# Tying weight stores, operand stores and the first operation of each weight conversion to their place in program order

## The chip, the cores and the metric

One core of one Trainium2 chip. The metric is the device time of one execution in microseconds (us), the median of three runs. PE is TensorE, DVE VectorE, ACT ScalarE, POOL GpSimd, SP SyncE, the engine whose only work here is to issue loads.

## The reference, cut to what matters

Three stages follow one another; 4 batches of 768 tokens are the 3072 rows of the last two.

```python
# 1: chunked attention, 8 heads of 64, chunk 32, left 16, right 8, 8 memory keys
scores = scale * q_c @ k_full.T ; a = softmax(scores) ; out = a @ v_full
# 2: x [3072,512], w_in [512,2048], w_out [2048,512]
h = x @ w_in ;  g = h * tanh(log1p(exp(h))) ;  x = g @ w_out
# 3: w_gate, w_val [512,1536], w_out2 [1536,512]
xn = x / sqrt(mean(x*x) + 1e-6) * rms_g
out = (silu(xn @ w_gate) * (xn @ w_val)) @ w_out2
```

The weights arrive as float64.

## The kernel before, in words

**Tiling.** The 3072 rows are 24 attention tiles of 128 rows. Three tiles make a block of 384 rows, two blocks a pair; there are four pairs. A product with `w_in`, or with `w_gate` and `w_val` together, is done for a pair at once by a 2x2 scheme with seven products (`group`, line 510). Its operands are seven tiles `T` per pair and seven parts of a weight slot. Every operand is split into a high and a low part (`split`, line 130: a copy on ACT, a subtraction on DVE or POOL), and each product is three matmuls for each of two contraction steps: 42 matmuls of 384 columns in a group.

**Weights.** A weight tile is loaded by SP as raw float64 halves (`load_raw`, line 119, two buffers `raw`) and converted by the generator `cv_all` (line 148). Its first two operations, lines 158 and 161, are on ACT and read `raw`; DVE goes on in lines 163 to 170. A job "pair" converts two tiles, forms sums on POOL and DVE, and splits into a slot; it has 11 steps. A job "rows" has 4 steps for each tile. `cv_upto(n)` advances the generator to step n at the places where the program calls it: 22 steps (two pairs, 4 tiles) while the first pair's attention is written down, to 55 in the 28 slots of the first four groups, to 88 in the next 56 slots, then none for 56 slots, to 152 in 84 slots, to 218 over the 64 steps of `out1`, to 284 and 332 in the last groups.

**Stages in time.** Attention of pair 0 (6 tiles, lines 342 to 443) comes first: no product exists before it. Then come 32 groups for `w_in` (line 551), where attention of pairs 1 to 3 lies between the products (`slots`, line 722), `out1` (64 steps of 24 matmuls, line 613), 48 groups for gate and value (line 561), and `out2` (line 663).

**Stores.** `w_store` (line 116, called by `keep_w`) writes a converted `w_in` slot to DRAM so that it can be loaded again for a later pair; the program places the eight stores in slots 1, 5, 14, 21, 30, 37, 44 and 51 of the second phase, which has the 56 slots of groups 4 to 11. `keep_x` (line 757) writes the seven `T` tiles of pair 0, in slots 8 to 20 of the first phase, groups 0 to 3. `store` (line 672) writes the result. Other stores go through `store_later` and `flush` (lines 92 to 99). All are issued from ACT's queue.

**What sets the order.** Each engine runs its instructions in one fixed order. That order isn't the one of the program text: a scheduler writes it when the kernel is built, from simulated times (`schedule_with_timeline_sim`, line 19). An instruction whose inputs are ready in that simulation may be put ahead of instructions that stand before it in the text.

Of the kernel before, what the change touches and what calls it, by code (L numbers as in the profile page):

```python
# [8 lines left out]
F32 = mybir.dt.float32  # L9
# [19 lines left out]
def tile_kernel(  # L29
# [13 lines left out]
    out: bass.AP,  # L43
):
    nc = tc.nc
    B, H, S, D = q.shape
    NMEM = mem_k.shape[2]
    NT, DM = out.shape
# [4 lines left out]
    N = 384  # L53
# [10 lines left out]
    wd = {("i", i): nc.dram_tensor(f"wi{i}", (128, SLOT), F32R, kind="Internal").ap()  # L64
          for i in range(F1 // 2)}
# [26 lines left out]
    def store_later(dst, src):  # L92
        late.append((tick[0] + 2, dst, src))

    def flush(all_=False):
        tick[0] += 1
        while late and (all_ or late[0][0] <= tick[0]):
            _, dst, src = late.pop(0)
            nc.scalar.dma_start(out=dst, in_=src)


    def w_slot(u):
        pool = w1p if u < NW1 else w2p[0]
        return pool.tile([128, SLOT], F32R, tag=f"w{u}", name="w")

    wtab, wslot = {}, {}

    def as7(s):
        return s.rearrange("p (a l f) -> p a l f", a=7, l=2)
# [4 lines left out]
        wtab[key] = as7(s)  # L114

    def w_store(key):
        nc.scalar.dma_start(out=wd[key].bitcast(F32), in_=wslot[key].bitcast(F32))

    def load_raw(arr, kind, f):
        raw = rawp.tile([128, 512, 2], I32, tag="raw", name="raw")  # L120
# [9 lines left out]
    def split(src, hi, lo, eng=None):  # L130
        nc.scalar.copy(hi, src)  # L131
        (eng or nc.vector).tensor_tensor(lo, src, hi.bitcast(F32), op=ALU.subtract)  # L132
# [3 lines left out]
    def add_pair(key, arr0, f0, arr1, f1, u, keep, store):  # L136
        jobs.append(("pair", key, [(arr0, "col", f0), (arr1, "col", f1)], u, keep, store))
# [4 lines left out]
    def cv_prefetch(done):  # L142
        flat = [part for job in jobs for part in job[2]]
        while n_load[0] < len(flat) and n_load[0] - done < 2:
            raws.append(load_raw(*flat[n_load[0]]))
            n_load[0] += 1

    def cv_all():

        done = 0  # L150
        for kind, key, parts, u, keep, store in jobs:
            tiles, slot = [], None
            for n in range(len(parts)):
                cv_prefetch(done)
                raw = raws.pop(0)
                a = cap.tile([128, 512], I32, tag="ca", name="ca")
                lr = cvp.tile([128, 512], I32, tag="lr", name="lr")
                nc.scalar.activation(
                    a.bitcast(F32), raw[:, :, 1].bitcast(F32), ACTF.Copy, scale=2.0 ** -112
                )  # L160
                nc.scalar.activation(lr, raw[:, :, 0].bitcast(U32), ACTF.Copy, scale=2.0 ** -29)
                yield
                nc.vector.tensor_scalar(a, a, 3, None, op0=ALU.logical_shift_left)
                nc.vector.scalar_tensor_tensor(  # L164
                    a, raw[:, :, 1], -2 ** 31, a, op0=ALU.bitwise_and, op1=ALU.bitwise_or
                )
                done += 1
                cv_prefetch(done)
                yield
                nc.vector.tensor_tensor(a, a, lr, op=ALU.add)  # L170
                yield
                a = a.bitcast(F32)
                if kind == "pair":
                    tiles.append(a)
                    continue
                if n == 0:
                    slot = w_slot(u)[:, 0:3 * 1024].rearrange("p (a l f) -> p a l f", a=3, l=2)
                w = slot[:, n]
                split(a, w[:, 0, :], w[:, 1, :], nc.gpsimd)
                wtab[key[n]] = w  # L180
                yield
            if kind == "rows":
                continue
            a0, a1 = tiles
            a11, a12, a21, a22 = a0[:, 0:256], a0[:, 256:512], a1[:, 0:256], a1[:, 256:512]
            sm = cvp.tile([128, 4, 256], F32, tag="sm", name="sm")
            s4, s1, s2, s3 = (sm[:, i, :] for i in range(4))
            nc.gpsimd.tensor_tensor(s1, a21, a22, op=ALU.add)
            nc.gpsimd.tensor_tensor(s3, a11, a21, op=ALU.subtract)
            slot = w_slot(u)  # L190
            w = as7(slot)
            def part(i, src):
                cnt = src.shape[-1] // 256
                src = src.rearrange("p (a f) -> p a f", f=256)
                split(src, w[:, i:i + cnt, 0, :], w[:, i:i + cnt, 1, :])
            part(0, a0)
            yield
            nc.vector.tensor_tensor(s2, s1, a11, op=ALU.subtract)
            nc.vector.tensor_tensor(s4, a12, s2, op=ALU.subtract)
            yield  # L200
            part(2, a22)
            yield
            part(3, sm[:, 0:2, :].rearrange("p a f -> p (a f)"))
            yield
            part(5, sm[:, 2:4, :].rearrange("p a f -> p (a f)"))
            if store:
                store_later(wd[key].bitcast(F32), slot.bitcast(F32))
            if keep:
                wtab[key], wslot[key] = w, slot
            yield  # L210
# [449 lines left out]
    def banks2(m):  # L660
        return [bk[(3 * m + r) % 8] for r in range(NSUB)]
# [10 lines left out]
    def store(m, n):  # L672
        for r, ps in enumerate(banks2(m)):
            o = cap.tile([128, 512], I32, tag="ca", name="o").bitcast(F32)
            if r % 2 == 0:
                nc.scalar.copy(o, ps)
            else:
                nc.vector.tensor_copy(o, ps)
            nc.scalar.dma_start(out=out[n * N + 128 * r:n * N + 128 * r + 128, :], in_=o)


    nc.scalar.preload_act_table_set("natural_log_exp_and_others")
# [16 lines left out]
    for f, u in zip(range(0, F2, 3), (7, 1, 2, 3)):  # L699
        fs = range(f, min(f + 3, F2))  # L700
        add_rows([("o2", x) for x in fs], w_out2, fs, u)
    cv[0] = cv_all()

    load_k(0, 0)
# [50 lines left out]
        return lambda: t_pieces(j, xb.pop(2 * j), xb.pop(2 * j + 1), t_new, None, ttab_x)  # L755

    def keep_x(p):
        return lambda: nc.scalar.dma_start(
            out=xt_d[:, p - 1].bitcast(F32), in_=ttab_x[0, p].bitcast(F32)
        )  # L760

    def keep_w(i):
        return lambda: w_store(("i", i))

    bt = slots((att_list(1), 28), (0, 55), tail_of(1),
               {8 + 2 * n: keep_x(p) for n, p in enumerate(ORDER)})
    for i in A:
        group1(0, i, bt)
# [51 lines left out]
    for s, (m, i) in enumerate(steps):  # L820
# [3 lines left out]
        if i == F1 // 2 - 1 and m < NB - 1:  # L824
            assert not pend
            n = order[m]
# [21 lines left out]
    def t_slot():  # L848
        if "x" not in hold:
            hold["x"] = w_slot(2)[:, 0:4 * N].rearrange("p (a b n) -> p a b n", a=2, b=2)  # L850
            return hold["x"]
        u = hold["n"] = hold.get("n", -1) + 1
        if u % 2 == 0:
            hold["s"] = w_slot(3)[:, 0:8 * N].rearrange("p (s a b n) -> p s a b n", s=2, a=2, b=2)
        return hold["s"][:, u % 2]

    p0, pend = rms_pieces(NB - 1, 1, t_slot)
    p0()

    def both():  # L860
        early, rest = t_pieces(0, xn.pop(0), xn.pop(1), t_slot, nt_d[0], {})
        pend.extend(early + rest)
# [41 lines left out]
    for s, (m, i) in enumerate(steps):  # L904
        t = feed.next(s)
        out2(m, i, t)
        if i == F2 // 2 - 1:
            store(m, order[m])
# [30 lines left out]
```

## Time and profile before

| | us |
|---|---|
| median of 3 runs (lowest, highest) | 1333.88 (1332.31, 1336.42) |
| the profiled execution's own time | 1333.24 |
| its span | 1331.5 |
| PE busy in the span | 1227.7 |
| DVE / ACT / POOL busy | 738.1 / 586.8 / 236.1 |

The span runs from the first to the last instruction of the profiled execution. A busy PE is not PE at its peak: matmuls are pipelined, so the count of matmuls in a stretch tells more than its busy time. "DMA share" is the mean busy share of the core's 16 DMA engines.

### The profile page before, as it was taken

The page shows a single profiled execution, that of the slowest core. Times are in us where ns is not written, and L with a number is a line of the kernel's source. Part 1 is how long each engine was busy: PE and PEld are TensorE (multiplying, and loading weights), DVE is VectorE, ACT ScalarE, POOL GpSimd, SP SyncE. Part 2 cuts the span into 40 slices and gives each one's busy share as a digit, 9 for nine tenths or more (in the row PEclk, how much of TensorE's full clock was granted, in tenths as well). Part 3 has the DMA queues.
Part 4 walks back from the last instruction along what each step waited for, and adds up shares of the span by engine and source line. Part 5 has one row for each costly group of instructions (what it writes and reads, how often), then busy time and mean ns, then how long its engine had stood idle before and what let it go on. Part 6 is the DMA issues. An engine that isn't in the chain of part 4 may idle for free.

```text
span 1331.5 us, 23277 instructions
## 1 busy us (share of the span) xinstructions
PE 1227.7 (92%) x9248; PEld 1134.2 (85%) x9248; DVE 738.1 (55%) x1276; ACT 586.8 (44%) x976; POOL 236.1 (18%) x197
## 2 busy tenths in 40 slices
PE   5559989999999879999999999989999999999998
PEld 3348778888899869989999999989999999888887
DVE  5666487363477577764656376955554337422220
ACT  4444355343354468757676344542432224322220
POOL 1002021020053311221212121311321114000000
PEclk9968889979999899999999999989999999999999
DMA  9998469669468697563636949858954553734321
GB/s 236 252 269 273 108 176 339 174 179 281 130 268 300 256 358 236 159 252 104 239 116 230 407 159 413 308 199 335 360 193 171 226 190 113 223 119 143 119 84 48
DMA packets 190637, 291.00 MB, mean 219 GB/s; under 512 B 103744, under 2 KB 152896, under 8 KB 186432
## 3 DMA queue, kind: packets, MB, share of 16 engines
q1 hardware_dynamic: 163600, 182.29, 43.5%
q10 hardware_dynamic: 26928, 107.23, 20.4%
q8 instruction: 72, 1.18, 0.4%
q14 instruction: 37, 0.30, 0.1%
HBM read 182.26 MB, written 107.22 MB: 217 GB/s over the span
## 4 chain that ended last, share of the span: by engine, by line
PE 48%; DMA 10%; DVE 6%; ACT 5%; issue 2%; POOL 1%; ACTq 0%; DVEq 0%; SPq 0%; POOLq 0%
PE bk L506 8%; PE bk L575 8%; PE bk L576 8%; PE bk L577 8%; PE bk L508 8%; PE bk L507 8%; DMA g<-g_scratch 3%; DMA T<-nt_scratch 3%; DVE T L132 2%; ACT T L131 1%; DMA T<-xt_scratch 1%; DVE ca L164 1%; ACT g L598 1%; DMA wg<-w 1%; DMA raw<-in_moe_w_out_dram 1%
## 5 line engine op out<-in xcount | busy, mean ns | idle before, releaser
L506 PE MATMUL bk<-T,w 128*128 128x384 f32 x1120 | 385.3, 348 | 21.1 <-DMA T<-nt_scratch 7.1
L507 PE MATMUL bk<-T,w 128*128 128x384 f32 x1120 | 383.7, 343 | 2.2 <-DVE T L132 2.1
L508 PE MATMUL bk<-T,w 128*128 128x384 f32 x1120 | 377.7, 342 | 0.0
L506 PEld LDWEIGHTS bk<-T,w 128*128 128x128 f32 x1120 | 215.1, 193 | 30.9 <-ACT s L568 6.3
L507 PEld LDWEIGHTS bk<-T,w 128*128 128x128 f32 x1120 | 215.0, 192 | 5.8 <-DVE T L132 4.7
L508 PEld LDWEIGHTS bk<-T,w 128*128 128x128 f32 x1120 | 214.5, 192 | 0.7
L132 DVE TENSOR_TENSOR T<-g,T 128x768 fp32r<-128x768 f32 x112 | 112.6, 1011 | 134.5 <-ACT T L131 134.1
L575 PE MATMUL bk<-T,w 128*128 128x384 f32 x512 | 169.8, 340 | 8.6 <-ACT T L131 8.6
L576 PE MATMUL bk<-T,w 128*128 128x384 f32 x512 | 174.1, 340 | 3.3 <-DVE T L132 3.3
L577 PE MATMUL bk<-T,w 128*128 128x384 f32 x512 | 172.5, 337 | 0.0
L131 ACT CAST T<-g 128x768 fp32r<-128x768 f32 x112 | 91.9, 835 | 108.2 <-PE bk L577 95.4
L575 PE MATMUL bk<-w,T 128*128 128x512 f32 x288 | 112.6, 391 | 0.0
L576 PE MATMUL bk<-w,T 128*128 128x512 f32 x288 | 112.5, 391 | 0.0
L577 PE MATMUL bk<-w,T 128*128 128x512 f32 x288 | 112.2, 391 | 0.0
L533 DVE TENSOR_TENSOR u<-bk,s 128x384 f32<-128x384 f32 x80 | 44.3, 553 | 112.1 <-PE bk L508 112.0
L575 PEld LDWEIGHTS bk<-T,w 128*128 128x128 f32 x512 | 96.2, 189 | 10.8 <-ACT T L131 10.2
L576 PEld LDWEIGHTS bk<-T,w 128*128 128x128 f32 x512 | 96.8, 189 | 6.8 <-DVE T L132 6.0
L577 PEld LDWEIGHTS bk<-T,w 128*128 128x128 f32 x512 | 96.6, 189 | 0.4
L537 POOL TENSOR_TENSOR v<-u,z 128x384 f32<-128x384 f32 x48 | 52.5, 1094 | 242.1 <-DVE u L533 200.4
L598 ACT ACTIVATE g<-g 128x768 f32<-128x768 f32 x64 | 53.6, 844 | 39.4 <-DMA g<-g_scratch 35.2
L537 POOL TENSOR_TENSOR g<-u,z 128x384 f32<-128x384 f32 x32 | 37.4, 1169 | 174.5 <-DVE u L533 142.2
L525 ACT COPY z<-bk 128x384 f32<-128x384 f32 x80 | 38.2, 477 | 67.9 <-PE bk L508 47.8
(116 smaller groups left out, 1654.5 us busy)
## 6 DMA issues: line engine op xcount, KB each, us to landing
T<-nt_scratch SPq DMA_DIRECT2D x56, 768.0 KB
g_scratch<-g ACTq DMA_DIRECT2D x64, 384.0 KB
g<-g_scratch SPq DMA_DIRECT2D x64, 384.0 KB
h_scratch<-s ACTq DMA_DIRECT2D x48, 384.0 KB
g<-h_scratch SPq DMA_DIRECT2D x48, 384.0 KB
nt_scratch<-T ACTq DMA_DIRECT2D x21, 768.0 KB
wi<-w ACTq DMA_DIRECT2D x8, 1792.0 KB
raw<-in_moe_w_out_dram SPq DMA_DIRECT2D x28, 512.0 KB
```

Source lines behind the costliest of these rows:

```text
L131: nc.scalar.copy(hi, src)
L132: (eng or nc.vector).tensor_tensor(lo, src, hi.bitcast(F32), op=ALU.subtract)
L506: nc.tensor.matmul(ps, whi, xh, start=first and kk == 0, stop=False, **more)
L507: nc.tensor.matmul(ps, whi, xl, start=False, stop=False, **more)
L508: nc.tensor.matmul(ps, wlo, xh, start=False, stop=kk == 1, **more)
L525: nc.scalar.copy(z5, z)
L533: nc.vector.tensor_tensor(u3, y, s1, op=ALU.add)
L537: nc.gpsimd.tensor_tensor(c22, u3, z5, op=ALU.add)
L575: nc.tensor.matmul(ps, ahi, bhi, start=start, stop=False)
L576: nc.tensor.matmul(ps, ahi, blo, start=False, stop=False)
L577: nc.tensor.matmul(ps, alo, bhi, start=False, stop=stop)
L598: nc.scalar.activation(g, g, self.act)
```

## The change

`tc.keep_in_program_order(ins)` adds one edge of order, without a wait, from the instruction that was written just before `ins` for the same engine: the scheduler may not put `ins` ahead of that one. Other instructions may still pass `ins`. It is put around the stores of `w_store`, `keep_x` and `store`, and around line 158. Besides, `t_slot`, which hands out buffers for the last normalised block's operands, now issues all pending stores before it takes a new buffer.

```diff
+    pin = tc.keep_in_program_order
...
     def w_store(key):
-        nc.scalar.dma_start(out=wd[key].bitcast(F32), in_=wslot[key].bitcast(F32))
+        pin(nc.scalar.dma_start(out=wd[key].bitcast(F32), in_=wslot[key].bitcast(F32)))
...
-                nc.scalar.activation(
+                pin(nc.scalar.activation(
                     a.bitcast(F32), raw[:, :, 1].bitcast(F32), ACTF.Copy, scale=2.0 ** -112
-                )
+                ))
...
-            nc.scalar.dma_start(out=out[n * N + 128 * r:n * N + 128 * r + 128, :], in_=o)
+            pin(nc.scalar.dma_start(out=out[n * N + 128 * r:n * N + 128 * r + 128, :], in_=o))
...
-        return lambda: nc.scalar.dma_start(
+        return lambda: pin(nc.scalar.dma_start(
             out=xt_d[:, p - 1].bitcast(F32), in_=ttab_x[0, p].bitcast(F32)
-        )
+        ))
...
         if u % 2 == 0:
+            flush(True)
             hold["s"] = w_slot(3)[:, 0:8 * N].rearrange("p (s a b n) -> p s a b n", s=2, a=2, b=2)
```

## Rows read from the trace of the kernel before

**Rows 1.** The page: busy us, share of the span and instructions of each engine.
```profile
PE 1227.7 (92%) x9248; PEld 1134.2 (85%) x9248; DVE 738.1 (55%) x1276; ACT 586.8 (44%) x976; POOL 236.1 (18%) x197
```

**Rows 2.** By stretch: length, PE PEld DVE ACT POOL busy (count), PE clock, DMA share, GB/s.
```profile
0.00:97.50 97.50, 51.64 (x885) 38.73 (x886) 62.16 (x144) 46.66 (x80) 11.25 (x21) 0.90 0.96 257
97.50:172.90 75.40, 68.13 (x1033) 57.38 (x1032) 39.31 (x98) 28.30 (x48) 8.16 (x5) 0.84 0.63 177
172.90:272.30 99.40, 90.76 (x1205) 80.56 (x1204) 64.74 (x147) 46.10 (x85) 18.20 (x14) 0.96 0.76 231
...
963.00:1130.00 167.00, 166.59 (x954) 165.54 (x955) 83.70 (x138) 55.42 (x114) 34.24 (x30) 1.00 0.48 181
```

**Rows 3.** Line 158 alone by stretch: stretch, length, ACT busy (times), clock, DMA.
```profile
0.00:97.50 97.50, 8.72 (x13) 0.90 0.96 257
97.50:172.90 75.40, 0.00 (x0) 0.84 0.63 177
...
363.50:469.50 106.00, 11.41 (x17) 0.94 0.73 273
469.50:514.20 44.70, 4.02 (x6) 0.96 0.92 340
514.20:625.00 110.80, 3.37 (x5) 1.00 0.52 174
625.00:759.00 134.00, 0.00 (x0) 1.00 0.64 235
```

**Rows 4.** Stores of lines 117 and 758: times, ns min/median/max, first and last start.
```profile
L117 ACTq DMA_DIRECT2D wi<-w x8: 326/327/372, 24.9 to 217.8; - x8
...
L758 ACTq DMA_DIRECT2D xt_scratch<-T x7: 326/326/327, 69.6 to 113.5; - x7
```

**Rows 5.** DMA from 0 to 97.5 us: queues (q1 loads, q10 stores), issues.
```profile
q1 hardware_dynamic: 37370, 14.99, 68.4%
q10 hardware_dynamic: 864, 9.96, 26.9%
...
wi<-w ACTq DMA_DIRECT2D x5, 1792.0 KB
raw<-in_moe_w_in_dram SPq DMA_DIRECT2D x15, 512.0 KB
```

**Rows 6.** What PE waited for, 0 to 97.5 us: total us, times, longest.
```profile
PE bk L292 <- DVE p L372: 10.9, 3, 5.8
PE bk L292 <- DMA kn<-in_k_dram: 8.6, 2, 4.9
PE bk L408 <- DMA vw<-in_v_dram: 4.9, 1, 4.9
```

**Rows 7.** One conversion's operations, whole span: busy us, mean ns, idle before.
```profile
L158 ACT ACTIVATE ca<-raw 128x512 f32<-128x512 f32 x68 | 45.4, 671 | 34.2 <-DMA raw<-in_moe_w_in_dram 11.0 <-DMA raw<-in_moe_w_out_dram 5.7 <-DMA raw<-in_moe_w_gate_dram 5.0
L161 ACT ACTIVATE lr<-raw 128x512 int32<-128x512 uint32 x68 | 45.3, 667 | 20.9 <-DVE ca L170 9.5 <-DMA raw<-in_moe_w_out_dram 5.1 <-DMA raw<-in_moe_w_in_dram 3.1
...
L132 DVE TENSOR_TENSOR w<-sm,w 128x512 fp32r<-128x512 f32 x40 | 28.7, 731 | 1.1 <-ACT w L131 0.8
...
L131 ACT CAST w<-sm 128x512 fp32r<-128x512 f32 x40 | 23.9, 617 | 18.1 <-DVE sm L198 16.3 <-DVE sm L199 1.7
```

**Rows 8.** `out1` from its first step, eight steps a row (columns as in Rows 2).
```profile
469.50:514.20 44.70, 37.45 (x193) 34.76 (x194) 34.90 (x54) 30.26 (x50) 6.54 (x7) 0.96 0.92 340
514.20:549.20 35.00, 34.52 (x195) 33.62 (x194) 29.01 (x47) 30.06 (x44) 8.23 (x9) 1.00 0.59 184
...
691.00:725.00 34.00, 34.00 (x196) 33.74 (x195) 24.99 (x29) 20.37 (x27) 9.22 (x5) 1.00 0.49 172
```

**Rows 9.** DMA issues from 469.5 to 514.2 us: count, KB each.
```profile
wg<-w ACTq DMA_DIRECT2D x4, 1792.0 KB
```

**Rows 10.** What PE waited for, 469.5 to 514.2 us: total us, times, longest.
```profile
PE bk L575 <- ACT T L131: 8.0, 3, 3.2
```

**Rows 11.** What PE waited for, 759 to 877 us: total us, times, longest.
```profile
PE bk L506 <- DMA T<-nt_scratch: 6.0, 3, 3.4
```

## The prediction

> **What bounds the kernel now.** I read the page first, then busy time by stretch, then, stretch by stretch, what PE waited for, where line 158 runs and what the DMA queues carry. The page shows PE 92% busy, with 104 us of the 1331.5 not busy [rows 1]. The stretches tell where: 45.9 us of those 104 lie in the first 97.5, while pair 0's attention runs and no product exists to fill PE; 7.3 in the next stretch, 8.6 in the third, 7.3 in the first eight steps of `out1` [rows 2, 8]. So the end is set by PE from 172.9 us on, but for short holes, and by the attention's own pace before that.
>
> The first two stretches each hold six tiles of attention. The second also holds most of four groups, yet takes 75.4 us against 97.5 [rows 2]. Two things set them apart. First, 13 conversions begin in the first and none in the second [rows 3]; the program text places 4 in the first and 6 in the second. Second, the DMA share is 0.96 against 0.63 [rows 2], and stores hold 26.9% of the first stretch's DMA time (five weight slots and a `T` tile, all placed later by the text), with 15 raw tiles loaded where the text needs 6 [rows 4, 5]. So the scheduler has floated work into the start, and there PE waits for attention's DVE work and for K and V loads [rows 6].
>
> **What the change does, part by part.** It removes no instruction; it moves them. Line 158 can't run ahead of the ACT instruction before it in the text, which in the first three stretches is mostly a copy out of PSUM that PE must have filled. The later steps of a tile hang on line 158, and the next raw load on the buffer that the tile frees, so both follow.
>
> *Part A, 0 to 97.5 us.* Out go 9 of 13 conversions, three weight-slot tails, 9 raw loads and all five weight stores. The difference to the next stretch is 97.5 - 75.4 = 22.1 us; I give half to the stores and half to the conversions, since PE's waits there are half on DVE and half on loads (10.9 against 8.6 + 4.9 [rows 6]). Stores: -11.0. Conversions: 11.0 x 9/13 = -7.6. The stretch becomes about 79 us. Bounds: nothing, if attention's own chain sets the pace; -30, if on top of these 18.6 the ACT time of 9 conversions, 9 x 1.34 = 12 us [rows 7], came off the path.
>
> *Part B, 97.5 to 172.9 us.* In come 6 conversions with three tails: 11.0 x 6/13 = +5.1. DVE has 39.3 us of work in 75.4, and had 22.9 more in the first stretch with 13 conversions [rows 2, 3]; six bring 6/13 of that, 10.5, so it isn't full. The `T` stores stay: they ran from 69.6 to 113.5 [rows 4] and move by some tens of us inside this stretch. Bounds 0 to +15.
>
> *Part C, 172.9 to 272.3 us.* In come the five weight stores, so that all eight lie here. 26.9% of 97.5 us is 26 us of DMA time, some 24 of it for the five; the share here is 0.76 of 99.4, or 75.5 [rows 2, 5]. Together 99.5 in 99.4: just full. PE has products to do meanwhile, so I charge +4; bounds 0 and +25 (the whole difference that a full DMA made in the first stretch, 22, and some of a weight slot that is ready only when its group begins). The last of them to be converted, slot 7 for group 11, now gets its parts right ahead of that group: four casts and four subtractions, 4 x 0.62 and 4 x 0.73 us in turns [rows 7], some 5 us that PE may have to wait, inside these bounds. Behind a store on ACT stands nothing that waits for its landing: it costs ACT 0.33 us, eight times [rows 4].
>
> *Part D, `out1`, 469.5 to 759 us.* The text spreads 12 conversions evenly over the 64 steps. Before, the counts are 6 in the first eight steps, 5 to 625 us, and none behind [rows 3]. In the first eight steps PE takes 44.7 us for what takes 34.0 late in the stage [rows 8]; it waits 8.0 us for the cast of the split [rows 10], at a DMA share of 0.92 with four `wg` stores [rows 8, 9] and the six conversions' raw loads. After the change one or no store and two raw loads fall there: 44.7 to about 36.5, so -8. The conversions that leave go to steps that have none now; eight steps with five conversions cost 35.0 against 34.0 [rows 8], so +2. Sum -6; bounds -10 and 0.
>
> *Part E, groups of gate and value.* Twelve conversions, now from 759 on, are spread evenly over 140 slots. PE waits 6.0 us there for `T` loads [rows 11], which share the DMA engines with the raw loads. I take -1, bounds -6 and +6: all of that wait, gone or doubled. The last six conversions come in the last 24 slots rather than earlier: +1, covered by PE that is full from 963 to 1130 [rows 2]. The pending stores issued early in `t_slot` can make ACT wait for a result of DVE a few times, 0 to +4; I take 0, as they may still be passed.
>
> *Part F, the rest.* The 24 result stores stand behind the copies that they need anyway, and an issue costs ACT about 0.33 us wherever it stands [rows 4]: 0. The stretch from 363.5 to 469.5 holds 17 conversions and by the text 16 [rows 3]: 0.
>
> Sum: -11.0 - 7.6 + 5.1 + 4 - 6 - 1 + 1 = -15.5 us. Against the profiled execution's own 1333.24 this gives 1317.7; the median of the runs, 1333.88, stands 0.6 higher, so 1318.
>
> **A rule of the skill that speaks against it.** The traffic argument rests on the first stretch's share of 0.96 and on PE's 4.9 us wait for V [rows 2, 6]. The Trainium skill ("DMA: Bandwidth & Descriptors", section "Rules for kernel authors") advises to issue a DMA early and wait on it late, so that its cost overlaps. By that rule the stores cost nothing where they are, the -11.0 of part A and the +4 of part C fall away, and the sum is -8.5, 1325 us. I side with the row, since a store that is early shares the engines with loads that attention waits for; the case lies in the forecast's own range below and has a fifth of its chance.
>
> **Rivals.** *More of the same.* Attention's pace without foreign work is faster than the 75.4 us stretch shows, since that stretch also did four groups: A -30, B +2, C 0, D -10, E 0, sum -38, 1295 us. For it: the tiles of pair 0 have ACT and DVE almost to themselves. Against: each tile's V load waits for the tile before.
>
> *Attention's own chain.* The floated work only filled holes. A and C 0, B +5, D -6: 1332 us. For it: DVE is busy 62 of 97.5 us, ACT 47 [rows 2]. Against: the next stretch is quicker with more to do.
>
> *Slower: the second phase takes over the full DMA.* Stores that were paid in the start are paid from 172.9 to 272.3, where loads for attention, weight reloads and `g` stores already run. It decides once the DMA share there stays over about 0.95, as in the start. C is then +22, B +10, A -18, D -6: +8, 1341 us. For it: 75.5 + 24 us fill the stretch. Against: PE has products there. The skill's "Issuing engines are not separate DMA queues" (same page) states that all issuers share the same 16 engines; by it nothing is gained by moving a store, only by when. The trace agrees: 68.4% and 26.9% make up the 0.96 [rows 5].
>
> *No effect.* The scheduler leaves the order as it was. Rows 3 and 4 against the text all but exclude it.
>
> **How the numbers follow.** Forecast 0.43, more of the same 0.19, own chain 0.13, slower 0.23, no effect 0.02. What can be told from no change is 0.3%, or 4 us. The forecast's own range is 1308 to 1328. The range from 1291 to 1345 holds all but the tails of the first and third rivals. Faster: 0.43 + 0.19 = 0.62. Same: 0.13 + 0.02, 0.15. Slower: 0.23.
>
> **What would show it.** Line 158 four or five times before pair 0's attention ends, and that end near 79 us; no `wi` store before about 140 us; the DMA share below 0.8 in the start and near 1 in the second phase; PE's wait for the cast in the first steps of `out1` down from 8.0 us to 2 or less. It is wrong if the start stays over 92 us, or if the gain in the start comes back as PE waits for K, V or weights before 272 us.

## The result and the profile after

The changed kernel takes 1302.64 us (median of 4, 1301.55 to 1305.15) against 1334.17 (4 runs beside it): a ratio of 0.9766, 95% interval 0.9744 to 0.9787. That is 31.5 us less, where 16 were forecast; it lies inside the stated range and between the forecast and the rival "more of the same". The profiled executions, 1333.24 and 1301.55 us, differ by 31.7. All kernels below were timed beside the kernel before. One execution of `e9_spread_stores`, 1965 us at a mean granted clock of 0.55, was in a slow state of the chip and is left out of its numbers.

Cut where the same work ends in both (last tile of each pair's attention, first product of each stage), the two traces compare so:

| work | before, us | after, us | difference | forecast |
|---|---|---|---|---|
| pair 0's attention (part A) | 97.5 | 70.2 | -27.3 | -18.6 |
| pair 1's attention, most of groups 0 to 3 (B) | 75.4 | 86.3 | +10.9 | +5.1 |
| pair 2's attention, most of groups 4 to 11 (C) | 99.6 | 111.4 | +11.8 | +4 |
| pair 3's attention | 91.0 | 90.8 | -0.2 | 0 |
| to `out1`'s first product | 106.1 | 100.3 | -5.8 | 0 |
| `out1`, first eight steps (D) | 44.6 | 35.4 | -9.2 | -8 |
| `out1`, rest (D) | 244.8 | 241.7 | -3.1 | +2 |
| first 14 groups of gate and value (E) | 119.0 | 111.3 | -7.7 | -1 |
| the other 34 groups | 252.1 | 251.1 | -1.0 | +1 |
| `out2` | 201.3 | 201.4 | +0.1 | 0 |

The start gained more than forecast, and the next two rows gave nearly all of it back: -4.8 by the end of attention. Profiled a second time (`e10_changed_again`), the changed kernel ended attention at 363.6 us, where the kernel before had 363.5: of the start's gain nothing is left that can be told from noise. The gain that lasts, 26.9 us, comes behind that. These are the stretches of the changed kernel, columns as in Rows 2, to be held against [rows 2] and [rows 8].

```profile
0.00:70.20 70.20, 51.03 (x886) 38.88 (x887) 36.68 (x99) 30.10 (x51) 4.91 (x13) 0.65 0.67 151
70.20:156.50 86.30, 71.25 (x1032) 59.18 (x1031) 57.77 (x132) 40.48 (x72) 14.03 (x11) 0.82 0.79 219
156.50:267.90 111.40, 94.14 (x1181) 83.32 (x1181) 66.23 (x148) 45.89 (x83) 19.08 (x16) 0.88 0.78 255
...
458.90:494.30 35.40, 34.17 (x195) 33.22 (x193) 19.26 (x28) 24.20 (x37) 3.83 (x4) 1.00 0.75 259
```

In the start DVE has 36.7 us of work instead of 62.2 and the DMA share is 0.67 instead of 0.96. Line 158 stands at 159 now. By stretch (length, ACT busy, times) it has the counts that the program text has, 4, 6 and 6, and is spread over `out1` [rows 3]; the stores of weight slots and operands start later [rows 4].

```profile
0.00:70.20 70.20, 2.66 (x4) 0.65 0.67 151
70.20:156.50 86.30, 3.87 (x6) 0.82 0.79 219
156.50:267.90 111.40, 4.03 (x6) 0.88 0.78 255
...
458.90:494.30 35.40, 1.48 (x3) 1.00 0.75 259
494.30:600.00 105.70, 3.37 (x5) 1.00 0.57 197
600.00:736.00 136.00, 3.35 (x5) 1.00 0.70 259
```

```profile
L118 ACTq DMA_DIRECT2D wi<-w x8: 326/326/1728, 142.4 to 268.0; - x8
```

```profile
L759 ACTq DMA_DIRECT2D xt_scratch<-T x7: 326/327/567, 85.1 to 131.8; - x7
```

PE's wait for the cast in the first eight steps of `out1` falls to 1.0 us. Of the 8.0 us before [rows 10], 3.1 end with the stage's first product and belong to the stretch ahead of it; 4.9 are the steps' own. In the changed kernel:

```profile
PE bk L576 <- ACT T L132: 1.0, 1, 1.0
```

And where 11.8 us were lost, in pair 2's stretch, one wait stands out: an attention transpose that waited 7.6 us for a copy on ACT.

```profile
PE bk L336 <- ACT pT L398: 7.6, 1, 7.6
PE bk L507 <- ACT z L526: 3.1, 1, 3.1
PE bk L409 <- DMA vw<-in_v_dram: 2.3, 2, 1.2
```

ACT's own order of time around it (start, us, what; in brackets the idle time before and what ended it) tells why:

```profile
177.49 0.81 ACTq L118 DMA_DIRECT2D wi<-w  x2
...
179.58 0.72 ACT L306 COPY kw<-bk 128x672 f32<-128x672 f32 x1 [0.45 <-DVE kw L302]
192.89 0.33 ACTq L100 DMA_DIRECT2D g_scratch<-g  x1
193.25 0.48 ACT L518 COPY s<-bk 128x384 f32<-128x384 f32 x1 [12.95 <-DMA kn<-in_k_dram]
193.35 0.34 ACTq L100 DMA_DIRECT2D g_scratch<-g  x1
193.74 0.59 ACT L398 COPY pT<-bk 128x512 f32<-128x512 f32 x1
```

Two tied stores of 1.8 MB went out back to back. After a few more operations ACT did nothing for 12.95 us: its next instruction, a store of `g`, was held until a load of K had landed. The store doesn't read K; in the trace it counts on the same semaphore as that load, and its own data was written by 183 us. The copy that PE needed stood behind it. The load was slow beside the two stores, as the queues (packets, MB, share) show for 181 to 189 us:

```profile
q10 hardware_dynamic: 243, 3.25, 95.8%
q1 hardware_dynamic: 227, 0.13, 5.2%
```

Loads and stores got about as many packets each, but a store's has 14336 bytes. Of the loads' 227, 125 had 256 bytes, as K's packets do, and 93, of 1024, belonged to a conversion's raw tile, issued 2 us ahead of the K load and in front of it in the queue. The Trainium skill ("DMA: Bandwidth & Descriptors", section "Queues, rings and completion order") says that each DMA engine takes turns between its queues packet by packet; 227 against 243 of the profile's packets agrees.

### The profile page after: what moved, and what is told of

It is laid out like the page before. It is cut to its first block, busy times and chain, and to the rows that moved or that the text cites. A ratio compares the mean times of both kernels' runs of the same rounds, so it can differ in the third digit from the quotient of the medians.

```text
span 1299.8 us, 23238 instructions
## 1 busy us (share of the span) xinstructions
PE 1224.3 (94%) x9248; PEld 1133.4 (87%) x9248; DVE 742.4 (57%) x1276; ACT 585.0 (45%) x976; POOL 225.2 (17%) x197
## 4 chain that ended last, share of the span: by engine, by line
PE 64%; DMA 14%; DVE 11%; ACT 6%; issue 3%; POOL 1%; SPq 1%; ACTq 0%; DVEq 0%; POOLq 0%
PE bk L507 12%; PE bk L508 11%; PE bk L509 11%; PE bk L577 8%; PE bk L576 8%; PE bk L578 8%; DMA T<-nt_scratch 4%; DVE T L133 4%; DMA vw<-in_v_dram 3%; DMA g<-g_scratch 3%; PE bk L409 2%; ACT T L132 2%; DMA kn<-in_k_dram 2%; PE bk L358 1%; DMA wi<-w 1%
## 5 line engine op out<-in xcount | busy, mean ns | idle before, releaser
L578 PE MATMUL bk<-w,T 128*128 128x512 f32 x288 | 111.5, 391 | 0.0
```

The costliest lines, as they stand in the source:

```text
L578: nc.tensor.matmul(ps, alo, bhi, start=False, stop=stop)
```

## The experiments

The theory at this point: tying the later conversions gives the lasting gain, by taking DMA traffic out of crowded places; tying the early ones and the stores moves the early loss about. The rivals: the stores did it; the start's gain lasts; it is the conversions' time on ACT and DVE. In the diffs `pin` is `tc.keep_in_program_order`, and `...` marks what is cut.

**Stores alone** (`e1_stores_only`).

```diff
-                pin(nc.scalar.activation(
+                nc.scalar.activation(
...
-            flush(True)
```

> Only the stores are tied (weight slots, pair 0's operands, result); line 158 floats as before. The halves of part A: if stores and conversions share the start's gain, pair 0's attention ends 97.5 -> about 87 us, and nothing changes after 363 us; with five stores moved to where group 4 to 11 run the total is 1325 to 1335 us. Rival, conversions alone made the start faster: the start stays at 95 to 98 us, total 1333 to 1345. Rival, the stores in the start were the whole of it: start about 72 us, total below 1320.

Measured: 1333.59 us, ratio 0.9972 (0.9947 to 0.9997). The start took 90.2 us, 7.3 less than before; 13 conversions had begun there by 65.7 us. Pair 2's stretch took 109.0 instead of 99.6. The stores alone freed some of the start and lost as much by the end of attention.

**Conversions alone** (`e2_conv_only`, again as `e11_conv_only_again`).

```diff
-        pin(nc.scalar.dma_start(out=wd[key].bitcast(F32), in_=wslot[key].bitcast(F32)))
+        nc.scalar.dma_start(out=wd[key].bitcast(F32), in_=wslot[key].bitcast(F32))
...
-            pin(nc.scalar.dma_start(out=out[n * N + 128 * r:n * N + 128 * r + 128, :], in_=o))
+            nc.scalar.dma_start(out=out[n * N + 128 * r:n * N + 128 * r + 128, :], in_=o)
...
-        return lambda: pin(nc.scalar.dma_start(
+        return lambda: nc.scalar.dma_start(
```

> Only line 158 is tied (and the early issue of pending stores kept); all stores float. My theory: the late gain (after 363 us, 26.9 us in the changed kernel) is all there; in the start only two weight slots are converted, so two stores fall into it, and the two stores that follow each other at 177 us in the changed kernel do not meet: pair 2's attention stretch 99 to 104 us instead of 111. Total 1292 to 1300 us. Rival, tying the stores is what freed the start: start 85 us or more, total 1305 to 1315.

Measured: 1296.53 us, ratio 0.9708 (0.966 to 0.9757). The start took 75.0 us, 22.5 less than before, with two weight stores in it, since a slot that isn't converted can't be stored; pair 2's stretch took 92.3, below the 99 to 104 expected. So the conversions, with their raw loads and the stores that follow them, are the larger part of the start's gain (-22.5, and -7.3 for the stores alone; together they gave -27.3).

**The late conversions alone** (`e3_conv_late_only`), with `cv_n[0]` the generator's step; 88 is the end of `w_in`. The stores of weight slots and operands float again (not shown); those of the result stay tied, and the early issue stays.

```diff
-                pin(nc.scalar.activation(
+                ins = nc.scalar.activation(
                     a.bitcast(F32), raw[:, :, 1].bitcast(F32), ACTF.Copy, scale=2.0 ** -112
-                ))
+                )
+                if cv_n[0] >= 88:
+                    pin(ins)
```

> Line 158 is tied only from the 17th tile on (the w_out, gate and value weights); the w_in conversions and all stores float as before. My theory: the start stays as before (pair 0's attention ends at 95 to 99 us, pair 3's near 363), and the late gain of some 27 us stands alone: 1304 to 1311 us. Rival, the late gain hangs on what the early order left behind (other loads, other buffers): less than half of it, 1320 to 1333 us.

Measured: 1303.28 us, ratio 0.9754 (0.9716 to 0.9792), the changed kernel's own time. Its first two attention stretches took 98.3 and 75.5 us, as before; the third 94.8 instead of 99.6, as three conversions of `w_out` that had run in it are gone from it; `out1` 275.3, the 14 groups 111.0. The late ties give the whole change. The result's stores have no part in it that shows: `out2` takes 201.3 or 201.4 us in every run.

**The early ties alone** (`e4_early_only`): the stores of weight slots and operands, and line 158 `if cv_n[0] < 88`.

> Line 158 is tied only for the 16 w_in tiles, with the stores of weight slots and operands; the later conversions float. My theory: the first 27 us won by pair 0's attention are given back by 363 us, to within 5 us, and nothing comes after: 1325 to 1333 us. Rival, the start's gain lasts to the end: 1305 to 1315 us.

Measured: 1328.19 us, ratio 0.9955 (0.993 to 0.9981). The start took 71.5 us, and 26.0 us less than before became 7.3 more by the end of attention (370.8 against 363.5). Of the start's gain at most a few us reach the end.

**Smaller packets for the slots** (`e5_small_packets`): the changed kernel with

```diff
-    wd = {("i", i): nc.dram_tensor(f"wi{i}", (128, SLOT), F32R, kind="Internal").ap()
+    wd = {("i", i): nc.dram_tensor(f"wi{i}", (7, 128, 512), F32R, kind="Internal").ap()
```

and store and reload written as `p a f`.

> The changed kernel with the DRAM copy of the w_in slots laid out in seven planes, so that their stores and reloads go in packets of 2048 bytes instead of 14336; the order of PE, DVE and POOL is the same. My theory: from 181 to 189 us in the changed kernel two stores that follow each other leave the 256-byte loads of K and V almost nothing, a store on ACT waits for one of these loads, and PE stands 7.6 us. With small packets the loads get their turns: pair 2's attention stretch 111.4 -> about 102 us, total 1291 to 1297 us. Rival, the DMA engines are full there whatever the packets' size: no change, 1299 to 1306 us.

Measured: 1306.99 us, ratio 0.9789 (0.976 to 0.9817); pair 2's stretch 111.5. The expectation fell. The loads did get more bytes, 0.80 MB in 11 us against 0.13 in 8, as the queues from 182 to 193 us show:

```profile
q10 hardware_dynamic: 1690, 3.41, 81.3%
q1 hardware_dynamic: 1738, 0.80, 25.2%
```

But the K load still landed only when the stores were nearly through, and PE's wait (line 336 is 344 here) was the same:

```profile
PE bk L344 <- ACT pT L406: 7.6, 1, 7.6
```

The trace shows why. From 186 to 192 us, with the raw tile through, the two queues moved as many packets each, K's of 256 bytes against stores' of 2048:

```profile
q10 hardware_dynamic: 1024, 2.06, 88.7%
q1 hardware_dynamic: 1018, 0.26, 19.0%
```

The K load has 1024 packets, the raw tile in front of it 512, and the two stores together 1792 of this size. Taking turns one for one, the load ends about when the stores do. What counted here was how many packets the load has, and how many it must take turns with.

**In conversions alone** (`e8_conv_only_small`) the same layout

> The kernel with only line 158 tied, with packets of 2048 bytes for the w_in slots. Its stores float and do not meet as in the changed kernel, so by my theory there is less to win: 1290 to 1296 us (1296.5 without). Rival, small packets make every slot transfer slower: 1297 to 1303 us.

gave 1302.23 us, ratio 0.9749 (0.9725 to 0.9773): no gain there either, and inside the rival's range.

**More traffic, or more work, at the head of `out1`.** Both start from `e3`. `e6_extra_traffic` adds a copy between DRAM arrays to each of the first eight steps; `e7_extra_compute` adds operations on a tile that nothing else uses.

```diff
+        if s < 8:
...
+            pin(nc.scalar.dma_start(out=xd[s], in_=flat.rearrange("(p f) -> p f", p=128)))
```

```diff
+        if s < 8:
+            for _ in range(3):
+                pin(nc.scalar.copy(dum[:, 0:256], dum[:, 0:256]))
+            for _ in range(4):
+                pin(nc.vector.tensor_tensor(dum[:, 256:512], dum[:, 256:512], dum[:, 256:512], op=ALU.add))
```

> The kernel with only the late conversions tied, with eight copies of 1.8 MB from one DRAM array to a scratch array added, one in each of the first eight steps of out1 (they are read by nobody). If DMA traffic was what the late conversions cost there before, the eight steps take 35.2 -> 41 to 46 us and the total rises by 6 to 11 us, to 1309 to 1315. If it was the conversions' time on ACT and DVE, they stay below 37 us and the total within 3 us of 1303.

> The kernel with only the late conversions tied, with three copies on ACT and four additions on DVE (128x256, on a tile that nothing reads) added to each of the first eight steps of out1, about what four more conversions cost there. If traffic was the cost, the eight steps stay below 37 us, total 1302 to 1306. If time on ACT and DVE was, 41 us or more, total 1308 to 1314.

Measured: 1330.95 us, ratio 0.9971 (0.9948 to 0.9994), with the copies, and 1306.89, ratio 0.9786 (0.9762 to 0.9811), with the operations. The eight steps in `e3`, `e6` and `e7`, in this order, columns as in Rows 2:

```profile
461.30:496.50 35.20, 34.12 (x194) 33.12 (x193) 19.23 (x28) 24.20 (x37) 3.83 (x4) 1.00 0.77 261
```

```profile
468.60:519.20 50.60, 36.05 (x194) 35.09 (x193) 18.61 (x27) 19.33 (x29) 4.89 (x4) 0.89 0.99 349
```

```profile
465.40:499.20 33.80, 33.56 (x194) 33.24 (x193) 29.02 (x54) 29.68 (x55) 4.41 (x4) 1.00 0.66 211
```

With DVE and ACT nearly as busy as before the change (29.0 and 29.7 us against 34.9 and 30.3 in a longer stretch, [rows 8]) the steps took 33.8 us: busy time on them that waits for nobody cost nothing. With the copies the steps took 50.6, more than expected, the rest of `out1` lost 16 us more, and the total lies far over the 1309 to 1315 expected: extra traffic can make the steps that long.

That traffic was the whole cost before the change does not follow. Before, the steps moved 340 GB/s x 44.7 us = 15.2 MB. In `e1` and `e4`, whose late conversions float too, the same eight steps moved 14.2 and 14.1 MB with the DMA engines full, and took 38.7 and 38.3 us (the stretch before them took 2.5 and 3.5 us more than before the change):

```profile
476.80:515.50 38.70, 37.15 (x194) 34.49 (x193) 30.86 (x48) 26.99 (x42) 7.00 (x8) 0.95 1.00 367
```

```profile
480.40:518.70 38.30, 36.41 (x194) 34.07 (x194) 30.93 (x48) 26.90 (x43) 7.07 (x8) 0.97 1.01 367
```

And ACT, whose cast PE waits for, did not wait for the same thing. First `e6`, then the kernel before:

```profile
ACT g L602 <- DMA g<-g_scratch: 24.3, 4, 14.3
```

```profile
ACT g L598 <- DMA g<-g_scratch: 3.5, 1, 3.5
ACT w L131 <- DVE sm L198: 3.2, 2, 1.7
ACT g L598 <- DVE ca L163: 2.9, 1, 2.9
```

Before the change ACT waited 3.5 us for a load of `g` and 9.7 us, in six waits, for DVE. PE's longest wait inside the steps, 3.2 us, ended with a cast that stood on ACT behind casts of a conversion, which had waited for DVE. So a rival is open: the conversions' own chain between ACT and DVE, in the order that ACT has them. The operations of `e7` stand in no such chain, and no run separates the two. That the late conversions cost there is shown; which of their ways of costing it was is not.

**The stores spread** (`e9_spread_stores`), beside the changed kernel and conversions alone.

```diff
-               {n: keep_w(i) for i, n in enumerate((1, 5, 14, 21, 30, 37, 44, 51))})
+               {n: keep_w(i) for i, n in enumerate((1, 7, 12, 22, 33, 40, 45, 51))})
```

> The changed kernel with the eight tied weight-slot stores put in slots 1, 7, 12, 22, 33, 40, 45 and 51 of the second phase instead of 1, 5, 14, 21, 30, 37, 44 and 51, so that in ACT's order at least eight rows lie between any two of them; the third and fourth stood two rows apart. My theory: two stores in flight at once are what starves the loads and stops ACT; spread, PE's 7.6 us hole near 187 us goes, pair 2's attention stretch falls from 111 to 95 to 103 us, total 1288 to 1295 us. Rival, tied stores cost there wherever they stand, by their bytes: 1299 to 1305 us.

> The changed kernel itself, beside the other two on the same chip: 1300 to 1305 us by every theory.

> Only line 158 tied, beside the changed kernel on the same chip: 1294 to 1299 us, 4 to 8 us below the changed kernel, if tying the stores costs; the same as the changed kernel if the first comparison was the chip's difference.

Measured: spread 1306.52 us, ratio 0.978 (0.9748 to 0.9812); the changed kernel 1301.98, 0.9766 (0.9739 to 0.9792); conversions alone 1299.2, 0.9748 (0.9723 to 0.9774). Spread, the hole is half as long and pair 2's stretch 105.7 us instead of 111.4 and 111.9, but the total shows none of it:

```profile
PE bk L409 <- DMA vw<-in_v_dram: 4.3, 2, 2.4
PE bk L336 <- ACT pT L398: 3.6, 1, 3.6
```

So two stores meeting is part of the price there, not all of it; how much of the rest is the stores' bytes stays open. Conversions alone was the lowest in both comparisons, by 6.1 us (in separate comparisons) and by 2.8, with intervals that overlap the changed kernel's; that it beats it is likely, not shown.

**`out1`'s conversions alone** (`e12_out1_only`): `e3` with `if 152 <= cv_n[0] < 218`.

> Line 158 is tied only for the 12 gate and value tiles that the text spreads over out1. If the late gain has three separate places, this has out1's alone: first eight steps 44.6 -> about 35 us, the stage from its first step to the first group of gate and value 289 -> 275 us, the groups from 759 to 878 us (119 us long before, 111 in the changed kernel) stay at 117 to 120, total 1313 to 1320 us. Rival, the groups' gain only follows from what out1 left behind: they take 110 to 113 us here too, total 1304 to 1310 us.

Measured: 1318.93 us, ratio 0.9869 (0.9826 to 0.9912). `out1` took 279.1 us (its first eight steps 33.3), and the stretch before it 100.2, as in the changed kernel: there gate and value tiles no longer run into the last `w_in` groups. The 14 groups behind took 118.3, with PE's wait for `T` loads (lines moved by 3) even above the 6.0 us of [rows 11]:

```profile
PE bk L509 <- DMA T<-nt_scratch: 8.5, 5, 3.6
```

In the changed kernel that wait is

```profile
PE bk L507 <- DMA T<-nt_scratch: 2.0, 4, 1.2
```

So the groups' gain is a place of its own. The traces place it more closely. Up to the twelfth group the kernel before and the changed kernel keep pace, 93.1 and 95.1 us; groups 13 and 14 took 25.9 us before and 16.2 after (columns as in Rows 2):

```profile
852.10:878.00 25.90, 19.70 (x86) 18.77 (x84) 13.84 (x23) 8.86 (x17) 3.90 (x4) 0.80 0.96 384
```

```profile
831.10:847.30 16.20, 15.24 (x86) 14.45 (x85) 8.24 (x14) 4.87 (x10) 1.03 (x2) 1.00 0.96 393
```

The DMA engines are full in both, at about the same rate, and before the change they had 9.9 MB to move there instead of 6.4. PE waited 5.6 us for `T` loads, and its granted clock fell to the lower of its two levels (1.2 and 2.4 GHz) after the first of the two waits and again in the second, for 10 us in all, with matmuls of 0.52 us instead of 0.34. Here the rows speak for traffic, though no run added any. `e12` also sizes the noise of the early part. Up to the last `w_in` groups its order on all engines is that of the kernel before, and its attention ended at 370.3 us, against 363.5: one execution's early part says nothing below some 7 us, and the changed kernel's -4.8 is less.

The early issue of stores in `t_slot` had no run: built without it, the changed kernel's order is the same on every engine.

## Why the prediction was right, and where its terms were off

The direction held, and so did the mechanism in outline: the scheduler had put conversions, raw loads and stores into crowded places, and the ties took them out. But the place where most of it was forecast, the start, gave nothing that lasts, and the places that gave the gain had been priced at little or nothing. That the total came within the range is in part luck. By its steps:

*Part A* was forecast as -11.0 for stores and -7.6 for conversions. Measured alone they give -7.3 and -22.5. The half-and-half split was the guess; the nine conversions with their DVE work, their raw loads and three stores that can't come before them weigh three times what I gave them. The bound of -30 held. The advice to issue early, weighed in the prediction, was read there as if a store's whole cost overlapped; the Trainium skill ("DMA: Bandwidth & Descriptors", section "Rules for kernel authors") says so of the fixed setup cost. In the start the stores did cost 7.3 us, and tying them alone gained nothing that lasts (`e1`).

*Part B*, +5.1, came to +10.9, inside its bounds.

*Part C*, +4, came to +11.8. Not by the rival's full DMA: the share of the stretch is 0.78, not over 0.95. Two stores met instead, a load of K, behind a raw tile in its queue, took turns with them, and a store of `g` that counts on that load's semaphore stopped ACT. I had written that nothing behind a store on ACT waits for its landing. That is the step that failed: the stores' own landing held nobody, but the load they slowed did. The mean share of a stretch hid it.

*Part D* was right in place and size for the first eight steps (-9.2 for -8). The cause it gave, traffic, is shown to be able to cost that much (`e6`), and `e1` and `e4` speak against it as the whole. Its 8.0 us of PE's wait were 4.9. The +2 for the later steps was -3.1: conversions beside a full PE cost nothing that shows.

*Part E* and *the stretch before `out1`* were undersized: -7.7 for -1, and -5.8 for 0. For the groups the waits for `T` loads were in the rows and I charged them as if moving raw loads wouldn't touch them; they fell from 6.0 us to 2.0, and PE's busy time for 592 matmuls, at a granted clock of 1.00 instead of 0.96, by 3.3 more. For the stretch before `out1` I compared counts of conversions, 17 against 16, and not which ones: the last four were gate and value tiles. The step that failed in both is the first one: of PE's 104 idle us the prediction listed 69, and the largest two places that this list left out are these, with 11.8 and 10.2 us:

```profile
363.50:469.50 106.00, 94.24 (x498) 90.71 (x498) 70.83 (x108) 52.65 (x96) 42.39 (x32) 0.94 0.73 273
759.00:878.00 119.00, 108.83 (x592) 106.66 (x590) 85.01 (x137) 54.58 (x103) 29.47 (x26) 0.96 0.78 306
```

*The signs.* Line 158 ran four times in the start, no `wi` store came before 142.4 us, the start's DMA share was 0.67, and the wait for the cast 1.0 us, as named. The start ended at 70.2 us, not near 79, and the share in the second phase was 0.78, not near 1. And the sign of being wrong came in substance: 22.7 of the start's 27.3 us were back by 268 us, 7.6 of them in a wait of PE that a load of K caused. Its row names ACT, since the load held ACT and ACT held PE.

So the size came out half of what was measured because the late stages were priced at less than a quarter of what they gave (-6 for -26.9), and attention's net, forecast at -9.5, was about nothing: with the late ties alone the total is the same.

## What to carry to other kernels

Where a scheduler orders by simulated times, look in the trace for work that runs long before its place in the program, and ask which transfers it brings along: tying one instruction moves its loads and stores too. List every stage in which the busiest engine idles before pricing any, and ask in each what its longest waits stand behind. Judge a gain by where the next common point of both traces ends, since a gain early can be gone two stages later. Large stores near each other, beside loads of many small packets, need a look at what else counts on those loads.

## What the hardware showed that was not expected

The clock column can look like an answer where it is none. Over the start the changed kernel has a mean granted clock of 0.65 and takes 70.2 us; `e9_spread_stores` has 0.98 and takes 71.0. It looks as if the clock did nothing.

```profile
0.00:71.00 71.00, 50.79 (x885) 38.38 (x886) 36.04 (x98) 30.11 (x50) 4.91 (x13) 0.98 0.66 148
```

The matmuls say otherwise. Attention's set of 64 took 1.61 us in the start of the changed kernel and of `e9_spread_stores`, and 0.91 us in the changed kernel at 179 us, where the granted clock is 1.00:

```profile
23.35 1.61 PE L409 MATMUL bk<-vw,pT 64*32 64x65 f32 x64
```

```profile
24.60 1.61 PE L409 MATMUL bk<-vw,pT 64*32 64x65 f32 x64
```

```profile
178.99 0.91 PE L409 MATMUL bk<-vw,pT 64*32 64x65 f32 x64
```

So both starts ran mostly at the lower level. The trace of `e9_spread_stores` has no entry of the clock before 57.9 us, and the column counts such time as full clock; the same goes for the 0.90 of [rows 2], where the entries begin at 71.5 us. Whether a faster clock would shorten the start, no run shows.
